# Sorting the second half of the keys' matrices ahead of the first scores, and fewer, wider warm-up matmuls

## The chip, the cores and the metric

The kernel runs on one core of one Trainium2 chip. A core has five engines with a queue of instructions each: TensorE (matmuls; the profile calls the matmuls PE and the loads of their stationary operand PEld), VectorE (DVE), ScalarE (ACT), GpSimd (POOL, which here also issues most of the loads) and SyncE (SP, which issues DMAs). They run side by side and wait for each other through semaphores. SBUF holds the working data, PSUM takes the results of matmuls. DMAs move data between HBM and SBUF; the engines' instructions too are fetched from HBM, by a DMA queue that the profile lists as "instruction".

The metric is the time of one execution in microseconds (us). Before the change it was 359.16 us, the median of 3 runs (359.14 to 359.62).

## The reference, cut to what matters

Four batches, 8 heads, 768 tokens in 8 blocks of 96, head size 64. A matrix of 8 x 8 for each batch and head is normalised five times over (Sinkhorn), then mixes the blocks of k and v; each block of queries attends to its own mixed block; the result goes through four experts of two layers whose outputs are summed with the token's weights.

```
P = sort_net
for _ in range(5):
    P = exp(P - max(P, -1)); P = P / sum(P, -1); P = P / sum(P, -2)
k_sorted = einsum('bhij,bhjcd->bhicd', P, k_b); v_sorted = the same of v_b
attn = softmax(scale * q_b @ k_sorted^T); x = attn @ v_sorted
out = sum over e of p[:, e] * (relu(x @ w1[e]) @ w2[e])
```

## The kernel before

The order of the work is written out by hand: the instructions of each engine run in the order in which the program emits them. The change lies in the first 15 us, the work on batch 0 up to the first experts.

**Warm-up.** `warm(n)` (L256) emits n matmuls of a constant tile `dummy` with itself, 128 columns each, whose result nobody reads. `warm(84)` stands first in TensorE's queue (L280). In the fifth round of the normalisation come the transposes of the first half of the queries (`h_q`, 2 x 24, L285 to 287), then `warm(30)` (L288). In the trace a matmul is a weight load and a matmul, two instructions.

**The sort matrices.** VectorE and ScalarE normalise `sn` in five rounds (L283 to 299). Then VectorE and GpSimd write a widened copy `sn16`, four of the eight block rows each (L303). `r_half(a)` (L314) turns one half by 4 matmuls against the identity into PSUM (`ps_R`, seen as `Rv`). For the first half VectorE at once builds the mixing operand `PI0[0]` from `Rv` (L354). The second half is needed as a copy in SBUF, `Rs`, from which GpSimd builds `PI0[1]` (L1375); later batches use `Rs` as well. `ps_R`, the warm-up tiles, `ps_mk` and others take turns in a pool of two PSUM buffers, so the second tile after `ps_R` (that of `mk1`) can't be written before `Rs` has been copied out.

**The first stage of batch 0.** Heads come in two quads (qd 0 and 1), output blocks in two halves (hf).

- `mix_half(nm, qd, hf)` (L485) mixes k or v by 24 matmuls; 8 keep-warm matmuls stand ahead of the first one (L481). `mixed` (L503) copies the product out, in two pieces for k of quad 0 (`mk0`: ScalarE, block rows 0-1 and 2-3) and v of quad 0 (`mv0`: VectorE).
- `h_s(qd, qq)` (L540): 8 matmuls of scores, then ScalarE's exponential into `ET` (L556).
- `h_w` (L517): transposes of mixed v, copied out by VectorE (L527).
- `h_a` (L561): 8 matmuls of attention times v; VectorE divides (L580, L581). With `later` the division is emitted afterwards.
- `h_x(qq, copy, qds)` (L590): 4 matmuls for each quad that turn the result into `xT`, and a copy out (L602).
- `group0(qq, nq, g, kcs)` (L666): the first expert's first layer, 16 matmuls of 192 columns for two kc; ScalarE's relu.

The program after the first half's `PI0` (L1365 on) is: mk0, its first copy, mv0, its first copy, `h_s(0, 0)`, `r_half(1)`, mk0's second copy on ScalarE, `Rs` on VectorE, GpSimd's loads and `PI0[1]`, `h_w(0)`, mv0's second copy, mk1 with two copies, `h_a(0, 0)`, `h_w` of the other two rows ("w01"), `h_s(0, 1)`, mv1, `h_x(0, [0])`, `h_s(1, 0)`, `h_w(1)`, `h_a(0, 1)`, `h_a(1, 0)`, the first `group0`, `h_w(1)` of the other rows ("w11"), `h_x(0, [1])`, and so on. From there to the end the experts' matmuls alternate with the attention of the later batches.

Of the kernel before, what the change touches and what calls it, by code (L numbers as in the profile page):

```python
# [17 lines left out]
def kernel(  # L18
# [11 lines left out]
    nc = tc.nc  # L30
# [8 lines left out]
    P = 128  # L39
# [27 lines left out]
    def psa(shape, dtype, name):  # L67
        state["n"] += 1
        return psA.tile(shape, dtype, tag="ps", name=name)
# [75 lines left out]
    def load_half_queries(hf):  # L145
        for qd in range(2):
            nc.gpsimd.dma_start(
                q0[ds(64 * qd, 64), hf].rearrange("p h r d -> p h (r d)"), half_queries(qd, hf)
            )

    dummy = Hflat[:, ds(2 * NFC * 2 * P, P)]
# [77 lines left out]
    def spread_weights():  # L229

        nc.vector.tensor_reduce(p_den, p_in, AX.X, ALU.add)
        yield
        nc.vector.tensor_scalar(out=p_den, in0=p_den, scalar1=1e-9, scalar2=None, op0=ALU.add)
        yield
        nc.vector.reciprocal(p_den, p_den)
        yield
        nc.vector.tensor_tensor(
            p_out.rearrange("p e t -> p t e"), p_in, p_den.broadcast_to([P, NT, E]), ALU.mult
        )
        p_rows = p_dram.rearrange("e (p t) -> p e t", t=NT)  # L240
        nc.sync.dma_start(p_rows[0:S_P], p_out[0:S_P])
        nc.sync.dma_start(p_0, p_dram[0, 0:S].rearrange("(t p) -> t p", p=P))
        pbs[(0, 0)] = load_p(0, 0)
        nc.sync.dma_start(p_rows[S_P:P], p_out[S_P:P])
        yield
# [10 lines left out]
    def warm(n):  # L256
        ps = psM.tile([P, 4, P], F32, tag="ps", name=f"ps_w_{state['n']}")
        state["n"] += 1
        for m in range(n):
            nc.tensor.matmul(ps[:, m % 4, :], dummy, dummy, start=True, stop=True)  # L260

    qT0 = [from_spare(2 * S).rearrange("p (s f r x) -> p s f r x", s=2, f=2, r=R) for _ in range(2)]

    def h_q(qd, hf, copy):

        ps = psa([P, 2, R, 64], F16, f"ps_q_{qd}_{hf}")
        rows = ds(64 * qd, 64)
        for sg in range(2):
            for r in range(R):
                for hh in range(2):  # L270
                    nc.tensor.transpose(
                        ps[ds(D * hh, D), sg, r, :], q0[rows, hf, 2 * sg + hh, r, :], ident[rows, rows]
                    )
        copy(qT0[qd][:, :, hf], ps[:])
# [2 lines left out]
    srow = const.tile([GH, NB, 1], F32, name="srow")  # L277
    scol = const.tile([GH, NB, 1], F32, name="scol")
    sn16 = const.tile([GH, NB, NB, CP], F16, name="sn16")
    warm(84)  # L280
    p_steps = spread_weights()
    nc.gpsimd.tensor_copy(ident6, ident[0:R, 0:R])
    for it in range(5):  # L283
        nc.scalar.activation(sn[:], sn[:], AF.Exp, bias=0.0, scale=1.0)
        if it == 4:  # L285
            for qd in range(2):
                h_q(qd, 0, nc.scalar.copy)
            warm(30)  # L288
        nc.vector.tensor_reduce(srow[:], sn[:], AX.X, ALU.add)
        nc.vector.reciprocal(srow[:], srow[:])  # L290
        nc.vector.tensor_tensor(sn[:], sn[:], srow[:].broadcast_to([GH, NB, NB]), ALU.mult)
        nc.vector.tensor_reduce(scol[:], sn[:].rearrange("p i j -> p j i"), AX.X, ALU.add)
        nc.vector.reciprocal(scol[:], scol[:])
        if it < 4:
            nc.vector.tensor_tensor(
                sn[:], sn[:],
                scol[:].rearrange("p j o -> p o j").broadcast_to([GH, NB, NB]),
                ALU.mult,
            )
            if it:  # L300
                next(p_steps)
# [10 lines left out]
    Rv = ps_R[:, :, 0:HB * GH].rearrange("p a (i g) -> p a i g", g=GH)  # L312

    def r_half(a):  # L314
        for i in range(HB):
            nc.tensor.matmul(
                Rv[:, a, i, :], sn16[:, a * HB + i, :, :].rearrange("g j c -> g (j c)"),
                ident[0:GH, 0:GH], start=True, stop=True,
            )
# [4 lines left out]
    Rs = const.tile([P, GH, NB], F16, name="Rs")  # L324
# [31 lines left out]
    vec, act = nc.vector.tensor_copy, nc.scalar.copy  # L356
# [128 lines left out]
    def mix_half(nm, qd, hf, pool, warm_up=0):  # L485

        ps = pool([P, 1024], F32, f"ps_m{nm}_{qd}_{hf}")
        keep_warm(ps[:, 0:P], warm_up)
        tails[(nm, qd, hf)] = ps[:, 2 * R * 64:1024].bitcast(F16).rearrange("p (n x) -> p n x", n=2)
        ps = ps[:, 0:2 * R * 64].rearrange("p (s r x) -> p s r x", s=2, r=R)  # L490
        for sg in range(2):
            for r in range(R):
                for hh in range(2):
                    h = 4 * qd + 2 * sg + hh
                    nc.tensor.matmul(  # L495
                        ps[ds(D * hh, D), sg, r, :],
                        head(0, nm, h)[:, r, :],
                        PI0[hf][:, h, :, :].rearrange("p i c -> p (i c)"),
                        start=True, stop=True,
                    )  # L500
        return ps

    def mixed(nm, qd, ps, i0, n, copy):  # L503

        dst = kTs[qd][:, 0:S] if nm == "k" else vT0[qd]
        copy(
            dst.rearrange("p (i x c) -> p x i c", i=HB, c=CP)[:, :, ds(i0, n)],
            ps.rearrange("p s r (i c) -> p (s r) i c", c=CP)[:, :, ds(i0, n)],
        )
# [30 lines left out]
    def h_s(qd, qq, ps=None):  # L540

        kT, ET = kTs[qd], ETs[2 * qd + qq % 2]
        if ps is None:
            ps = psa([P, 2, 512], F32, f"ps_s0_{qd}_{qq}")
        for n in range(4):
            for hh in range(2):
                sg, i = n // 2, 2 * (qq % 2) + n % 2

                m = BLK if 2 * i + sg == 3 else P
                nc.tensor.matmul(  # L550
                    ps[0:m, hh, ds(n * BLK, BLK)],
                    kT[ds(D * hh, D), ds((2 * i + sg) * BLK, m)],
                    qT0[qd][ds(D * hh, D), sg, qq // 2, :, ds((2 * (qq % 2) + n % 2) * CP, CP)],
                    start=True, stop=True,
                )
        nc.scalar.activation(  # L556
            ET[:, 0:S].rearrange("c (h x) -> c h x", h=2), ps[0:BLK, :, 0:HS],
            AF.Exp, bias=0.0, scale=SCALE,
        )
# [806 lines left out]
    mixed("k", 0, mk0, 0, 2, act)  # L1366
    mv0 = mix_half("v", 0, 0, psa)
    mixed("v", 0, mv0, 0, 2, vec)
    h_s(0, 0)
    r_half(1)  # L1370
    mixed("k", 0, mk0, 2, 2, act)
    vec(Rs.rearrange("p g (a i) -> p a g i", a=2), Rv.rearrange("p a i g -> p a g i"))
    load_half_queries(1)
    load_w2(0, 2)
    build_PI0(nc.gpsimd, 1, 0, H, Rs[:, 0:H, HB:NB])  # L1375
# [160 lines left out]
```

## Time and profile before

| what | before |
|---|---|
| median of 3 runs | 359.16 us (359.14 to 359.62) |
| profiled execution: from its first to its last instruction (span) | 357.8 us |
| profiled execution: its own time | not listed beside its span; the runs' median is 1.3 us above the span |
| TensorE matmuls, weight loads | 3949 and 3949 |
| TensorE busy | 351.6 us, 98% of the span |
| packets of the instruction queue q8 | 31, together 0.51 MB |
| granted TensorE clock | full from 5.99 us, not granted in full before |

A timeline line reads: start, duration, engine, line of the program, operation, output tile <- input tiles, shape, count, and in brackets how long the engine sat idle before it and what ended that. A matmul's duration includes its run through the array, so rows of matmuls overlap. "issue" as a releaser means that no semaphore and no engine shown by the profile explains the idle time.

### The profile page before, as it was taken

The page shows a single profiled execution, that of the slowest core. Times are in us where ns is not written, and L with a number is a line of the kernel's source. Part 1 is how long each engine was busy: PE and PEld are TensorE (multiplying, and loading weights), DVE is VectorE, ACT ScalarE, POOL GpSimd, SP SyncE. Part 2 cuts the span into 40 slices and gives each one's busy share as a digit, 9 for nine tenths or more (in the row PEclk, how much of TensorE's full clock was granted, in tenths as well). Part 3 has the DMA queues.
Part 4 walks back from the last instruction along what each step waited for, and adds up shares of the span by engine and source line. Part 5 has one row for each costly group of instructions (what it writes and reads, how often), then busy time and mean ns, then how long its engine had stood idle before and what let it go on. Part 6 is the DMA issues. An engine that isn't in the chain of part 4 may idle for free.

```text
span 357.8 us, 9498 instructions
## 1 busy us (share of the span) xinstructions
PE 351.6 (98%) x3949; PEld 306.3 (86%) x3949; DVE 276.2 (77%) x552; ACT 170.6 (48%) x303; POOL 133.6 (37%) x149
## 2 busy tenths in 40 slices
PE   8899999999999999999999999999999999999996
PEld 8686867888888888888899988888888888888886
DVE  5754797869889587868978988896678886588963
ACT  2554240442434535367947258830288611688201
POOL 8864010375122222000535318840058800188400
PEclk9999999999999999999999999999999999999999
DMA  8999999999999999935996420005200015100011
GB/s 114 207 205 228 216 210 198 209 163 165 201 154 160 188 152 170 194 74 73 168 201 90 102 78 0 2 2 108 102 29 2 3 39 138 61 0 2 2 73 46
DMA packets 72022, 40.51 MB, mean 113 GB/s; under 512 B 40614, under 2 KB 66732, under 8 KB 71980
## 3 DMA queue, kind: packets, MB, share of 16 engines
q0 software_dynamic: 36576, 19.93, 41.9%
q1 hardware_dynamic: 35260, 19.92, 28.5%
q8 instruction: 31, 0.51, 0.6%
q14 instruction: 11, 0.09, 0.1%
q10 hardware_dynamic: 144, 0.07, 0.1%
HBM read 42.13 MB, written 6.34 MB: 135 GB/s over the span
## 4 chain that ended last, share of the span: by engine, by line
PE 95%; DVE 2%; ACT 1%; DMA 0%; issue 0%; DVEq 0%
PE ps_h L790 18%; PE ps_Q L1264 18%; PE ps_p L774 12%; PE ps_X L1121 10%; PE ps_Z L1121 7%; PE ps_Q L1121 7%; PE ps_Z L1264 6%; PE ps_h L679 3%; PE ps_o L714 3%; PE ps_p L830 3%; PE ps_a L453 2%; PE ps_s L418 2%; PE ps_k L399 1%; PE ps_v L365 1%; PE ps_a L567 1%; PE ps_mk L495 1%
## 5 line engine op out<-in xcount | busy, mean ns | idle before, releaser
L790 PE MATMUL ps_h<-xT,w 128*128 128x256 f16 x576 | 67.5, 273 | 0.0
L790 PEld LDWEIGHTS <-w 128*128 128x128 f16 x576 | 55.2, 98 | 7.2
L796 DVE SCALAR_TENSOR_TENSOR Hb<-ps_h,pb 128x1024 f16<-128x1024 f32 x34 | 41.5, 1223 | 17.2 <-PE ps_h L790 15.8
L1121 PEld LDWEIGHTS <-w 128*128 128x128 f16 x480 | 43.6, 98 | 4.8
L1134 POOL TENSOR_TENSOR arena<-tmp,pb 128x512 f16<-128x512 f32 x12 | 15.2, 1275 | 65.7 <-PE ps_Z L1121 49.8
L1264 PEld LDWEIGHTS <-Hb 128*128 128x128 f16 x320 | 31.1, 98 | 3.5
L1133 ACT ACTIVATE tmp<-tmp 128x512 f32<-128x512 f32 x46 | 29.0, 632 | 3.9 <-DVE tmp L1171 3.9
L1264 PEld LDWEIGHTS <-Sb 128*128 128x128 f16 x304 | 28.3, 98 | 3.0
L1121 PEld LDWEIGHTS <-arena 128*128 128x128 f16 x312 | 27.7, 98 | 2.9
L425 ACT ACTIVATE ET<-ps_s 96x768 f16<-96x768 f32 x24 | 18.0, 802 | 25.1 <-PE ps_s L418 24.8
L121 POOL DMA_DIRECT2D arena<-in_q_dram x24 | 19.9, 838 | 25.5 <-DMA q_ring<-arena 25.2
L408 ACT CAST kT<-ps_k 64x384 f16<-64x384 f32 x48 | 22.7, 473 | 13.3 <-PE ps_k L399 12.3
L1121 PE MATMUL ps_X<-ET,arena 128*128 128x256 f16 x168 | 25.2, 272 | 0.0
L1264 PE MATMUL ps_Q<-w,Hb 128*128 128x256 f16 x192 | 24.6, 273 | 0.0
L774 PEld LDWEIGHTS <-Hb 128*128 128x128 f16 x232 | 21.8, 98 | 3.0
L1127 DVE SCALAR_TENSOR_TENSOR Hb<-ps_X,pb 128x512 f16<-128x512 f32 x27 | 18.7, 691 | 7.0 <-PE ps_X L1121 7.0
L1141 ACT COPY ps_X<-ps_Z 128x512 f32<-128x512 f32 x27 | 15.4, 571 | 17.8 <-PE ps_Z L1121 17.8
L1121 PE MATMUL ps_Z<-xT,w 128*128 128x256 f16 (+1 forms) x176 | 22.5, 258 | 0.0
L760 DVE TENSOR_TENSOR Sb<-Hb 128x512 f16<-128x512 f16 x33 | 20.6, 647 | 0.0
L1148 ACT COPY tmp<-ps_X 128x512 f32<-128x512 f32 x26 | 15.2, 585 | 9.2 <-PE ps_X L1121 6.6
L1127 DVE SCALAR_TENSOR_TENSOR Hb<-ps_Z,pb 128x512 f16<-128x512 f32 x27 | 18.4, 682 | 1.3 <-PE ps_Z L1121 1.3
L1171 DVE TENSOR_TENSOR tmp<-ps_Q,tmp 128x512 f32<-128x512 f32 x26 | 17.8, 683 | 0.8 <-PE ps_Q L1121 0.8
(266 smaller groups left out, 741.6 us busy)
## 6 DMA issues: line engine op xcount, KB each, us to landing
w<-in_moe_w_dram POOLq DMA_DIRECT2D x6, 1024.0 KB, 27.9
pb<-p_dram SPq DMA_DIRECT2D x9, 512.0 KB, 7.0
arena<-in_k_dram POOLq DMA_DIRECT2D x8, 384.0 KB, 9.3
arena<-in_v_dram POOLq DMA_DIRECT2D x8, 384.0 KB, 7.5
vs<-arena SPq DMA_DIRECT2D x36, 66.0 KB, 4.9
arena<-in_q_dram POOLq DMA_DIRECT2D x24, 96.0 KB, 7.5
out_dram<-ob SPq DMA_DIRECT2D x9, 256.0 KB, 2.0
w<-in_moe_w_dram POOLq DMA_DIRECT2D x4, 512.0 KB, 12.5
```

The lines of the kernel that those rows point to most:

```text
L121: nc.gpsimd.dma_start(t[:, h // 2, :, h % 2, :], q[b, h].rearrange("(t p) d -> p t d", p=P))
L408: nc.scalar.copy(kT[ds(D * hh, D), r], pk[ds(D * r, D), hh].rearrange("p a (i c) -> p a i c", c=CP),)
L425: nc.scalar.activation(ETs[2 * (pr % 2) + hh][:, 0:S].rearrange("c (a x) -> c a x", a=2), pss[hh][0:BLK, :, 0:HS], AF.Exp, bias=0.0, scale ...
L760: tt(sm[0], blk(0, 1), blk(1, 1), ALU.add)
L774: nc.tensor.matmul(ps, lhs(e, f), Ts[e][rhs][:, f, :], start=(first and e == es[0] and f == 0), stop=(done and e == es[-1] and f == KH - 1 ...
L790: nc.tensor.matmul(ps[:, f, :], w1sb[e][:, kc, ds((4 * g + f) * P, P)], xT[:, kc, ds(2 * c * P, 2 * P)], start=(kc == 0), stop=(kc == NKC ...
L796: nc.vector.scalar_tensor_tensor(out=Hb[:, homes.get(e, e), ds(4 * g, 4), :], in0=ps[:], scalar=0.0, op0=ALU.max, in1=weights(e).broadcast ...
L1121: nc.tensor.matmul(dst[:, ds(f * cols, cols)], a[lhs][:, k, ds((f0 + f) * P, P)], t[rhs][:, k, :], start=(first and f == 0 and k == 0), st ...
L1127: nc.vector.scalar_tensor_tensor(out=home(i, j), in0=src.rearrange("p (f x) -> p f x", f=m), scalar=0.0, op0=ALU.max, in1=weight(j).broadc ...
L1133: nc.scalar.activation(src, src, AF.Relu, bias=0.0, scale=1.0)
L1171: tt(t12, Q, u2, ALU.add)
L1264: nc.tensor.matmul(ps, lhs(e, f), Ts[e][rhs][:, f, part], start=(first and e == 0 and f == 0), stop=(e == E - 1 and f == KH - 1), skip_gro ...
```

## The change

`warm` emits matmuls of 512 columns: the moving operand is the same tile of 128 columns, read four times over, and the output is the whole buffer of 4 x 128. It is called with 21 and 8 instead of 84 and 30. `r_half(1)` moves ahead of `h_s(0, 0)` in TensorE's queue. The copy `Rs` moves from VectorE, where it stood behind mv0's first copy, to ScalarE, where it stands between mk0's first copy and the exponential of `h_s(0, 0)`. GpSimd's queue and SyncE's are as before.

```
         for m in range(n):
-            nc.tensor.matmul(ps[:, m % 4, :], dummy, dummy, start=True, stop=True)
+            nc.tensor.matmul(
+                ps[:], dummy, dummy.rearrange("p (o x) -> p o x", o=1).broadcast_to([P, 4, P]), start=True, stop=True
+            )
...
-    warm(84)
+    warm(21)
...
-            warm(30)
+            warm(8)
...
     mixed("v", 0, mv0, 0, 2, vec)
+    r_half(1)
+    act(Rs.rearrange("p g (a i) -> p a g i", a=2), Rv.rearrange("p a i g -> p a g i"))
     h_s(0, 0)
-    r_half(1)
     mixed("k", 0, mk0, 2, 2, act)
-    vec(Rs.rearrange("p g (a i) -> p a g i", a=2), Rv.rearrange("p a i g -> p a g i"))
     load_half_queries(1)
```

## The prediction

> **What bounds the kernel now.** First the page: busy shares and the chain.
>
> ```profile
> PE 351.6 (98%) x3949; PEld 306.3 (86%) x3949; DVE 276.2 (77%) x552; ACT 170.6 (48%) x303; POOL 133.6 (37%) x149
> ...
> q8 instruction: 31, 0.51, 0.6%
> ...
> PE 95%; DVE 2%; ACT 1%; DMA 0%; issue 0%; DVEq 0%
> ```
>
> TensorE bounds. The waits of TensorE from 20.3 us to the end hold one row, the stall that ends at 20.27:
>
> ```profile
> PE ps_s L522 <- issue: 0.2, 1, 0.2
> ```
>
> So after 20.3 TensorE runs without a gap, and what its queue is late or early there, the end is. The change can only count ahead of that. TensorE's timeline there:
>
> ```profile
> 8.97 1.85 PE L260 MATMUL ps_w<-Hb 128*128 128x128 f16 x30
> 11.79 0.26 PE L316 MATMUL ps_R<-ident,sn 32*128 32x32 f16 x4 [0.98 <-DVE sn L304]
> ...
> 13.78 0.21 PE L550 MATMUL ps_s<-Sb,kT 64*128 64x96 f16 x1 [0.19 <-ACT kT L506]
> 14.17 0.33 PE L550 MATMUL ps_s<-Sb,kT 64*128 64x96 f16 x7 [0.18 <-issue]
> ...
> 17.23 0.34 PE L598 MATMUL ps_a<-perm,xsl 96*128 96x96 f16 x4
> ...
> 19.85 0.22 PE L522 MATMUL ps_s<-ident,Sb 128*96 128x128 f16 x1
> 20.27 0.37 PE L522 MATMUL ps_s<-ident,Sb 128*96 128x128 f16 x3 [0.20 <-issue]
> 20.47 0.34 PE L598 MATMUL ps_a<-perm,xsl 96*128 96x96 f16 x4
> ```
>
> The warm-up ends in an idle second: r_half(0) waits for VectorE. Two stalls of 0.39 and 0.41 us (13.78 to 14.17, 19.85 to 20.27) stand within groups whose data are there: "issue". Numbering TensorE's records in order of time, they fall behind the 449th and the 705th, 256 apart. The 31 packets of q8 hold 16.4 KB each, and 31 x 256 is nearly all of TensorE's 7,945 records. So I read: instructions come in blocks of 256, the first boundary is behind record 193 (in the query transposes, at 8.37 us), and the stalls are blocks that come late. The DMA packets confirm it: q8's start at 11.786, 17.861 and 23.894 us and take 0.95, 0.94 and 0.97. The stalls end 1.44 and 1.47 us after the first two have ended, and the second and third start 3.69 and 3.63 us after the stalls have ended. So: on entering a block TensorE asks for the one after it, no earlier, and that can be used 3.66 + 0.95 + 1.45 = 6.06 us later. Thirty-one crossings and 31 packets fit two blocks being there at the start.
>
> The Trainium skill (Runtime: NRT & Kernel Launch, Instruction fetch mechanics) states blocks of 256 instructions too, fetched while the one before runs, and crossing "mostly hidden". The two stalls here were not hidden. By that rule alone the sum below would be that of the first rival, 358.7 us.
>
> **The change part by part.**
>
> *Warm-up.* 114 pairs of weight load and matmul become 29: 85 pairs, 170 instructions, go. Columns stay: 84 x 128 = 21 x 512, and 30 x 128 = 3,840 against 4,096. The trace starts these matmuls every 0.107 us until the clock is granted at 5.99 us, then every 0.056; a 512-column one of the second layer starts every 0.216 when warm, and cold it should take 4 x 0.107 = 0.43. From 1.06: 11.6 cold, 9.4 warm, end at 8.03 instead of 8.09. The eight take 1.73 instead of 1.68. The idle second until 11.79 takes both: 0. Bounds: no gain, since VectorE ends that wait; no loss until the clock comes some 2 us later (each us of half speed costs half a us), which nothing in the trace suggests at equal columns.
>
> *The boundaries.* Everything behind the warm-up stands 170 records earlier in its blocks. The first boundary falls behind old record 363, mk0's seventh load. mk0's first matmul waits for VectorE's PI0 (released at 12.60), so TensorE crosses at about 12.68, not during the warm-up as before (11.79 less 3.66 is 8.1). That it cannot run ahead through a wait: twice in the trace a sequencer record eight instructions behind a waiting one (17.150 and 67.002 us) came 0.05 us after that one's release (17.102, 66.955), though its own semaphore had long come. The next block is then usable at 12.68 + 6.06 = 18.74. It is needed behind old record 619, inside h_x(0, [0]): in program order its third load is the last of the old block, and its third matmul (17.32 us in the trace) starts at 18.74: **+1.42**.
>
> The Trainium skill (Perfetto Trace Analysis, Tensor Engine Instruction) has matmuls wait in a hardware queue while the sequencer goes on. If that queue were deep, the crossing would come about 11.8 at r_half(0) or before; that is the second rival or the first.
>
> *What is queued behind.* h_x's copy on ScalarE (17.61, 0.48), then exp of h_s(1, 0) (starts 0.375 behind the copy's start, released 0.82 later), h_a(1, 0), VectorE's division (0.96 from h_a's release), h_x(0, [1]). These are the rows of ScalarE's and VectorE's timelines:
>
> ```profile
> 17.61 0.48 ACT L602 CAST xT<-ps_a 128x384 f16<-128x384 f32 x1
> 17.98 0.81 ACT L556 ACTIVATE ET<-ps_s 96x768 f16<-96x768 f32 x1
> ...
> 18.48 0.42 DVE L527 COPY Sb<-ps_mv 96x512 f16<-96x512 f16 x1 [0.26 <-PE ps_mv L522]
> 19.39 0.20 DVE L580 RECIPROCAL rz<-ps_a 96x8 f32<-96x8 f32 x1 [0.49 <-PE ps_a L567]
> 19.63 0.69 DVE L581 TENSOR_TENSOR xsl<-ps_a,rz 96x512 f16<-96x512 f32 x1
> ```
>
> The fourth matmul, at 17.365 before, comes at 18.78 and is released at 19.00; copy 19.03; exp 19.40, released 20.22; h_a(1, 0) 20.27 instead of 18.95: +1.31 (0.1 less, since VectorE's evacuation, 18.91 before, no longer comes last). The division ends 1.31 later; h_x(0, [1]) then follows it directly, where it stood 0.05 behind: +1.26 at old 20.47. The old stall at 19.85 goes, but the division (old 20.33) lay over it: 0.07 of the 0.41, counted here. First weights' second half lands at 21.18, needed at 21.68 and now later: 0.
>
> *Next boundaries.* Third: entered 18.74, usable 24.80; needed behind old record 875, in h_x(1, [1]) at old 24.68, now 25.94: hidden. The next is asked for there: usable 25.94 + 6.06 = 32.00, needed behind old record 1131, a 512-column matmul of the second layer whose successor, at old 30.44, is due at 31.70: **+0.30**. Then: asked for at 32.0, usable at 38.1, needed at old 39.9: hidden. From 45 us on the packets are 7 to 17 us apart, more than 6.06: 0 (0 to 0.2).
>
> *The reorder.* r_half(1) needs GpSimd's sn16, released at 12.66; it can run behind mv0 (13.6) where TensorE idles 0.19: 0. Rs on ScalarE: nearest rows 0.48 (128x384 from PSUM there) and VectorE's own 0.42 for the same copy; by size 0.39, bounds 0.26 (a 32x64 activation) and 0.48. It delays exp(0, 0) by up to that against a first score without its stall: exp would start 14.33 instead of 14.54. mk1 no longer waits 0.23 for VectorE's Rs. Without late blocks h_x(0, [0]) would be reached 0.42 us sooner: mv0's first copy ends at 14.19, so h_w(0) could start at 14.25 instead of 14.62 and VectorE's evacuation of it at 14.73 instead of 15.15; mv0's second copy, w01, h_s(0, 1), mv1 and h_x follow each other from there (17.23 to 16.8). With the block usable at 18.74 all this ends in the same wait: 0. GpSimd's PI0[1] needs Rs by 15.39, when its loads are issued, and Rs is there by 14.5: 0. No DMA is moved.
>
> Sum: 1.26 + 0.30 = 1.56 us. The profiled execution's span goes from 357.8 to 359.4; the median of the runs stands 1.3 above that span: 359.16 + 1.56 = **360.7**.
>
> **The rivals.**
>
> 1. *Blocks are in time* (other side). If TensorE crosses by 10.7 us, during the warm-up, the block is usable at 16.8, when h_x(0, [0]) is reached. Then the 0.39 at 13.78 goes, the reorder brings h_x 0.42 forward, and from 20.3 it stays: 358.7 (358.4 to 359.1). For it: records run up to 34 ahead in steady stretches. Against: the two records held behind a wait. It decides up to 10.7 (16.8 less 6.06); from 11.2 the wait has eaten the 0.42.
> 2. *Crossing at r_half(0)*: 34 ahead of execution, record 159 is reached at 11.8. Usable 17.9, +0.6 in h_x, 0.42 at 20.47, 0.3 at the later boundary: 359.9 (359.6 to 360.1).
> 3. *A crossing costs a fixed 0.4, whenever.* Then one in mk0 replaces that of h_s(0, 0); one in h_x is mostly seen (0.1 to 0.3), one at old 24.7 (0.35), and 0.07 is won: 359.6 (359.2 to 359.9). Against: at 19.85 the load's data had come at 19.42, and a fixed 0.4 would have been over by 19.87.
> 4. *The clock falls* in the longer wait of 1.5 us: half speed for some us, +1 to 3. Against: after the idle 0.98 at 10.8 the keep-warm matmuls of 11.99 still start 0.056 apart.
>
> **How the numbers follow.** Chances: late blocks as worked out 0.62, rival 1 0.16, 2 0.12, 3 0.06, 4 0.04. The likeliest one's own range: the asking lag was 3.63 and 3.69, and 4.05 if the first crossing ran 34 ahead; 3.43 and 3.78 for the next two: +1.0 to +1.65 for the first, 0.05 to 0.55 for the second wait: 360.2 to 361.4. The range reaches down over rivals 2 and 3 to the middle of rival 1: 358.7 to 361.4. A measurement of this kernel tells about 0.2%, 0.72 us, from no change: slower is above 359.88 (0.62 less a little, a third of rival 2, rival 4: 0.68), faster below 358.44 (rival 1's edge: 0.05), same 0.27.
>
> **What would show it.** Warm-up rows x21 and x8, ending near 8.2 and 10.9. q8's first packet near 16.3 us instead of 11.8, the second near 22.4, the third near 29.7. No issue stall at h_s(0, 0); one of some 1.5 us inside h_x(0, [0]) ending near 18.7; none at the w11 transposes; a short one near 32 in the second layer; no gap behind. h_x(0, [1]) near 21.8. First packet at 12 to 14 us and no stall: rival 1. Wrong also, if the compiler gave TensorE a few more or fewer instructions, which moves the boundary out of h_x (by up to five either way it stays).

## The result, and the profile after

The changed kernel takes 360.86 us (median of 22 runs, 360.34 to 362.48); the kernel before, beside it on the same chip, takes 359.62 (22 runs, 359.14 to 361.97). The ratio is 1.0035, with a 95% interval of 1.0023 to 1.0046: slower by about 1.24 us. The fastest executions differ as much: 360.34 against 359.14. The forecast was 360.7. Of all executions named below, one, with 58 pairs, took 518 us at a granted clock of 0.66 and is left out.

The profiled execution of the changed kernel took 361.94 us, 1.78 above its span of 360.16. The later profiles have 1.77 to 1.86 between span and time too. So the profiled execution of before, with its span of 357.84, took about 359.62, and the prediction's base of 359.16 belonged to faster executions than the one it had read.

First the page of the changed kernel: busy shares, the instruction queue, the chain.

```profile
PE 352.0 (98%) x3864; PEld 301.6 (84%) x3864; DVE 276.1 (77%) x551; ACT 171.0 (47%) x304; POOL 133.7 (37%) x149
...
q8 instruction: 30, 0.49, 0.6%
...
PE 92%; DVE 3%; DMA 2%; SPq 1%; issue 1%; ACT 1%; DVEq 0%
```

85 matmuls and 85 loads are gone, and one code packet with them. TensorE is still 98% busy, but the chain now holds 2% of DMA and 1% of SPq, where before it had neither to speak of. What DMA that is comes below. TensorE's timeline, up to the second transposes (start, duration, line, operation, tiles, count, idle before):

```profile
1.06 6.35 PE L260 MATMUL ps_w<-Hb 128*128 128x512 f16 x21 [1.06 <-DVE Hb L152]
...
8.12 1.90 PE L260 MATMUL ps_w<-Hb 128*128 128x512 f16 x8
11.73 0.26 PE L318 MATMUL ps_R<-ident,sn 32*128 32x32 f16 x4 [1.71 <-DVE sn L306]
...
16.77 0.26 PE L600 MATMUL ps_a<-perm,xsl 96*128 96x96 f16 x2
18.26 0.32 PE L600 MATMUL ps_a<-perm,xsl 96*128 96x96 f16 x2 [1.23 <-issue]
...
21.97 0.34 PE L600 MATMUL ps_a<-perm,xsl 96*128 96x96 f16 x4
```

The stall is where the prediction put it: h_x(0, [0]) starts its first two matmuls at 16.77, and the third waits for nothing but its own instruction until 18.26. q8's first three packets start at 15.77, 22.06 and 29.00 us. The two stalls of before are gone. h_x(0, [1]) runs at 21.97, 1.50 us later than at 20.47 before.

Part of those 1.50 us is the clock. The same execution by stretches (start:end, length, busy time and count of each engine, granted clock, DMA share, GB/s):

```profile
core 0: us, PE busy (x) PEld busy (x) DVE busy (x) ACT busy (x) POOL busy (x), PEclk, DMA share, GB/s
...
18.00:21.50 3.50, 3.24 (x39) 2.97 (x39) 0.93 (x3) 1.72 (x3) 1.48 (x4) 0.51 1.20 204
21.50:24.00 2.50, 2.50 (x41) 2.26 (x39) 1.83 (x5) 1.19 (x2) 2.23 (x4) 1.00 1.25 207
```

The granted clock is half from 18.07 us, 0.19 ahead of the end of the stall, to 21.49, then full again. At the third matmul the lag is 0.94 (17.32 before, 18.26); with the slower clock it is 1.54 when the old transposes of 20.27 run. And there is a wait that before does not have anywhere behind 20.3 us; the waits of TensorE from 20.3 us to the end:

```profile
PE ps_a L455 <- DMA vs<-arena: 0.4, 1, 0.4
```

It ends at 181.18 us and takes the lag to 2.05. `vs` is a tile of mixed v for a later batch. ScalarE copies the product out into a part of `arena` (L371 before, L373 after), SyncE (SP) moves it into `vs` by six DMAs (L379, now L381), and TensorE multiplies with it (L453, now L455). The span is longer by 2.32 us, 0.30 more than the lag of TensorE's last matmul; where that comes from, the run with the new order alone shows.

### The profile page after: what moved, and what is told of

Same layout as the page of the kernel before. It is cut to its first block, busy times and chain, and to the rows that moved or that the text cites. A ratio compares the mean times of both kernels' runs of the same rounds, so it can differ in the third digit from the quotient of the medians.

```text
span 360.2 us, 9329 instructions
## 1 busy us (share of the span) xinstructions
PE 352.0 (98%) x3864; PEld 301.6 (84%) x3864; DVE 276.1 (77%) x551; ACT 171.0 (47%) x304; POOL 133.7 (37%) x149
## 4 chain that ended last, share of the span: by engine, by line
PE 92%; DVE 3%; DMA 2%; SPq 1%; issue 1%; ACT 1%; DVEq 0%
PE ps_h L792 18%; PE ps_Q L1266 17%; PE ps_X L1123 10%; PE ps_p L776 10%; PE ps_Z L1123 7%; PE ps_Q L1123 7%; PE ps_Z L1266 6%; PE ps_h L681 3%; PE ps_o L716 3%; PE ps_p L832 3%; DMA vs<-arena 2%; PE ps_a L455 1%; PE ps_s L420 1%; PE ps_k L401 1%; SPq L381 1%; PE ps_v L367 1%
## 5 line engine op out<-in xcount | busy, mean ns | idle before, releaser
L1266 PE MATMUL ps_Q<-w,Hb 128*128 128x256 f16 x192 | 24.6, 273 | 0.0
L1173 DVE TENSOR_TENSOR tmp<-ps_Q,tmp 128x512 f32<-128x512 f32 x26 | 17.8, 683 | 0.8 <-PE ps_Q L1123 0.8
```

The lines of the kernel that those rows point to most:

```text
L1173: tt(t12, Q, u2, ALU.add)
L1266: nc.tensor.matmul(ps, lhs(e, f), Ts[e][rhs][:, f, part], start=(first and e == 0 and f == 0), stop=(e == E - 1 and f == KH - 1), skip_gro ...
```

## The experiments

All twelve runs compute the whole reference; the warm-up matmuls that some of them add give results that nobody reads. Shifts below are starts of the same TensorE instruction in the new profile less its start in the first profile of before. "h_x(0,[1])" is at 20.47 there. Batches of runs had their own runs of the kernel before beside them; its median was 359.5 to 359.6 each time.

### One half of the change at a time

Only the warm-up, in the old order:

```
-                nc.tensor.matmul(ps[:, m % 4, :], dummy, dummy, ...)
+                nc.tensor.matmul(ps[:], dummy, <dummy read four times over>, ...)
...
-    warm(84)
+    warm(21)
...
-            warm(30)
+            warm(8)
```

> Only the warm-up of the change (21 and 8 matmuls of 512 columns), the order of the sort matrices as before. Theory 'late block': the whole loss is here. TensorE enters its second block of instructions only in the first mix at about 12.66 us, the next block can be used 5.6 to 6.1 us later, and a stall without a data reason ends between 18.2 and 18.8 us inside h_x(0, [0]); before + 0.9 to 1.4 us, no issue stall at the first scores. Rival 'order': the loss comes from Rs standing on ScalarE ahead of the first exponential, then this kernel is as before (within 0.2 us). Rival 'clock': the loss is a fall of the granted clock in the wait; then the loss goes with the record of the clock (0.6 us where it falls for 3.4 us, else nothing beyond the stall).

Measured: 360.97 us, ratio 1.0034 (1.0016 to 1.0052). TensorE's timeline in h_x, then its waits from 20.3 us on:

```profile
16.85 0.26 PE L600 MATMUL ps_a<-perm,xsl 96*128 96x96 f16 x2
17.72 0.24 PE L600 MATMUL ps_a<-perm,xsl 96*128 96x96 f16 x2 [0.61 <-issue]
...
20.68 0.34 PE L600 MATMUL ps_a<-perm,xsl 96*128 96x96 f16 x4
```

```profile
PE ps_a L455 <- DMA vs<-arena: 1.1, 1, 1.1
PE ps_s L420 <- ACT arena L373: 0.3, 1, 0.3
```

The warm-up alone carries the whole loss. But the stall is only 0.61 us here and leaves 0.21 at h_x(0,[1]); the clock stays full. Most of this execution's lag comes later: it goes to 0.70 at 162.15 us, where ScalarE's copy into `arena` is late, and to 1.92 at 181.05, where `vs` is late.

Only the new order, with the 114 matmuls of 128 columns as before:

```
     mixed("v", 0, mv0, 0, 2, vec)
+    r_half(1)
+    act(Rs...)
     h_s(0, 0)
-    r_half(1)
     mixed("k", 0, mk0, 2, 2, act)
-    vec(Rs...)
```

> Only the order of the change, with the 114 warm-up matmuls of 128 columns of before. Theory 'late block': the boundary behind record 449 now lies in r_half(1), its stall ends at about 14.2 us as before, the next one again at the w11 transposes at about 20.2 us, where TensorE waited before too; so before + 0.0 (-0.1 to +0.2 us). Rival 'order': before + 0.9 to 1.4 us.

Measured: 359.74 us, ratio 1.0006 (0.9992 to 1.0021). Neither of the two stalls on issue that were expected is there; h_x(0,[0]) starts at 16.85, and h_x(0,[1]) at 20.00:

```profile
20.00 0.34 PE L598 MATMUL ps_a<-perm,xsl 96*128 96x96 f16 x4
```

h_x(0,[1]) is 0.47 early, and TensorE's last matmul is still 0.45 early; yet the span is 357.94, not shorter. In this execution the time from VectorE's last addition to the end, with the last write of the output, was 0.55 longer than in the first profile of before. The second queue of code, q14, has one packet more within the span, and the last write took longer from its issue to its landing (lines of the page and of the view of that write, in us); first before, then the new order:

```profile
q14 instruction: 11, 0.09, 0.1%
...
DMA to landing us min/median/max: 1.6/1.6/1.6
```

```profile
q14 instruction: 12, 0.10, 0.1%
...
DMA to landing us min/median/max: 2.2/2.2/2.2
```

This is no chance of one execution. In all eight profiles with the new order a packet of q14 starts 1.26 to 1.41 us after the start of TensorE's last matmul, while that write is under way, the write takes 1.9 to 2.2 us, and the end comes 3.65 to 3.99 us after that start. In all six with the old order that packet starts only after the end of the span, the write takes 1.6, and the end comes after 3.38 to 3.42. ScalarE has one instruction more in the new order (304 against 303, `Rs`), which would move a boundary of its code; that this is what brings the packet forward, and the packet what delays the write, is argued and not shown. So the order gains 0.45 us in front and loses 0.55 at the end, and in the sum nothing can be measured.

### How many instructions: 89, 58 and 42 pairs

In these the warm-up keeps about its time, but some matmuls stay at 128 columns, so that fewer instructions go. Sketch for 89 pairs in the new order (`warm(n, wide)` emits n of 128 columns and then `wide` of 512):

```
-    warm(84)
+    warm(59)
...
-            warm(30)
+            warm(22, 8)
```

> The order of the change, with 89 warm-up matmuls instead of 29 or 114: 59 of 128 columns first, then 22 of 128 and 8 of 512, so about the same columns and the same time. Theory 'late block': the first boundary is crossed at about 7 us, the next block can be used at about 13, and is needed inside mk1 at about 14.6: no issue stall there; the one after is asked for at about 14.7, can be used at 20.3 to 20.8 and is needed at about 21: none or under 0.1 us. No issue stall at all ahead of 25 us, TensorE reaches h_x(0, [1]) at about 20.0 us instead of 20.47, before - 0.45 us (-0.6 to -0.2). Rival 'order': slower than before by 0.9 to 1.4 us, since the order is that of the change. Rival 'width': between before and the change.

> The order of before with the 89 warm-up matmuls of the run with the new order. Theory 'late block': no issue stall either, before - 0.4 us (-0.55 to -0.15); the new order by itself is worth 0.05 us (mk1 no longer waits for Rs, but the chain over VectorE's copies of mixed v is hardly shorter). If the order were worth more, this kernel would be 0.2 us or more behind the one with the new order.

89 pairs in the new order: 360.01 us, 1.0012 (1.0000 to 1.0024). In the old order: 359.53, 0.9997 (0.9981 to 1.0012). A gain of 0.4 us and more was expected of both, and neither shows it. Neither has a stall on issue up to 24 us. The profile of the first has other waits instead: 0.39 us for the v load before 13.61, 0.31 for the first weights before 22.26. That v load is issued at 4.04 to 4.13 us in every kernel, and landed between 10.8 and 13.6 us over the profiles.

Then the two that should find the edge:

```
-    warm(21)
+    warm(30, 14)      # 58 pairs       warm(16, 17)   # 42 pairs
...
-            warm(8)
+            warm(9, 5)                 warm(2, 7)
```

> The changed kernel with 58 warm-up pairs in place of 29: 30 of 128 columns and 14 of 512 in the first group, 9 and 5 in the second, about the same time in all. 112 TensorE instructions fewer than in the kernel before, so the first boundary lies at the third pair of the second group, crossed at about 8.5 us. Late block: with the lags seen so far (2.6 to 3.9 us until the block's first packet, 0.95 for it, up to 1.6 until it can be used) the next block can be used by 13.7 to 15.0 us and is needed at about 16.1; the one behind it is needed at about 23.1 and there by 22.5. No wait on issue between 12 and 24 us, time 359.6 to 360.1 beside 359.5 for the kernel before. If it is the wide matmuls themselves (the clock, or what 512 columns do to it) that cost, 19 of the 29 are still there and it takes 360.3 to 360.9. If the loss grows evenly with the number of instructions taken away, 112 of 170 give 0.7 to 0.9 us: 360.2 to 360.4.

> The changed kernel with 42 warm-up pairs in place of 29: 16 of 128 columns and 17 of 512 in the first group, 2 and 7 in the second. 144 TensorE instructions fewer than in the kernel before: the first boundary lies two pairs behind the last of the four transposes of r_half(0), crossed at 11.9 to 12.1 us, since that one waits for VectorE's sn until 11.73. Late block: usable at 17.2 to 18.5 us, needed at about 16.5 in the mix of mv1: a wait on issue of 0.7 to 1.5 us there, in another tile than in the changed kernel, and 360.2 to 361.0 us. If TensorE's sequencer reads past the waiting transpose by tens of instructions, the boundary is crossed at about 10.7, the block is there by 16.9 and the wait is under 0.4 us, 359.6 to 360.0. If the loss grows evenly with the number of instructions taken away: 144 of 170 give 1.0 to 1.2 us with no wait on issue in one place.

58 pairs: 360.87 us (11 runs), ratio 1.0044 (1.0025 to 1.0063). 42 pairs: 360.50, 1.0023 (1.0014 to 1.0032). Neither matches the theory of the late block. The times alone speak for its rivals: by the intervals 58 pairs lose 0.9 to 2.3 us, where the wide matmuls were given 0.7 to 1.3 and a loss that grows with the instructions taken away 0.7 to 0.9, and 42 pairs lose 0.5 to 1.15, where the latter was given 1.0 to 1.2. With 58 pairs the front is as good as it gets (h_x(0,[1]) at 19.99, 0.48 early, no stall on issue), and the kernel is as slow as the changed one. TensorE's waits from 20.3 us on, with 58 pairs:

```profile
PE ps_h L794 <- DVE Hb L800: 0.5, 1, 0.5
PE ps_s L422 <- ACT arena L375: 0.2, 1, 0.2
```

The lag goes from -0.48 to +0.24 at 98.06 us and to +0.68 at 162.12, and the end with the last write is 0.56 longer than before. At 98 us VectorE had waited for a 512 KB load (pb) of SP's queue, which landed at 96.69 (96.29 before). So there is a loss that needs no stall in front. With 42 pairs there is no stall on issue at all; q8's first packet starts at 11.62 us, 0.18 before r_half(0) runs. The new block begins 11 instructions behind r_half(0)'s waiting first load, and in the other 13 profiles the first packet started 2.5 to 3.9 us after the instruction at the boundary ran; here 0.44 before. So TensorE had asked for it before the wait was over: it does read at least 11 instructions past a waiting one. What this execution waits for is loads:

```profile
16.68 0.57 PE L499 MATMUL ps_mv<-Sb,arena 128*64 128x64 f16 x24 [0.26 <-DMA arena<-in_v_dram]
...
21.91 0.83 PE L683 MATMUL ps_h<-xT,w 128*128 128x192 f16 x8 [0.30 <-DMA w<-in_moe_w_dram]
```

### The two kernels once more

No edit; second profiles.

> The changed kernel once more, for a second profile of it. Late block: a wait on issue of 0.8 to 1.4 us ahead of the third matmul of h_x(0,[0]), at about 17.3 of the kernel before, with the granted clock full throughout, and h_x(0,[1]) 0.6 to 1.0 us later than in the kernel before; 360.3 to 360.7 us where vs<-arena is in time at 181 us and 1.1 us more where it is not. If the fall of the clock is part of the change, it is there again from about 18 us and adds 0.5 us at h_x(0,[1]).

> The kernel before once more, for a second profile of it, to see what of a shift between two profiles is in neither's edit. Waits on issue at the same two records, 13.8 to 14.2 and 19.9 to 20.3 us, h_x(0,[1]) within 0.2 us of the first profile, no wait for vs<-arena at 179 us or one of up to 1.1 us, since some runs of this kernel take 1.1 to 1.7 us more than its median.

The changed kernel: 361.39 us (5 runs, 360.85 to 361.81; ratio 1.0043, 1.0028 to 1.0058). Its timeline and its waits from 20.3 us on:

```profile
17.70 0.24 PE L600 MATMUL ps_a<-perm,xsl 96*128 96x96 f16 x2 [0.60 <-issue]
...
20.66 0.34 PE L600 MATMUL ps_a<-perm,xsl 96*128 96x96 f16 x4
```

```profile
PE ps_s L420 <- ACT arena L373: 0.7, 1, 0.7
PE ps_a L455 <- DMA vs<-arena: 0.3, 1, 0.3
```

The same stall in the same place, but of 0.60 us where the first profile had 1.23. It leaves +0.19 at h_x(0,[1]); the clock does not fall. The lag then goes to 1.10 at 162.55 and 1.60 at 180.73. The fall of the clock is no fixed part of the change: of the 22 runs only the profiled one has a mean clock below 0.998, and two of the 35 runs of the kernel before that stood beside the first four experiments have 0.994 and 0.995.

The kernel before: one run, 359.50. It has neither of the two stalls on issue from which the prediction read the blocks; q8's first packet starts at 11.42 instead of 11.79, and that is enough. It waits 0.34 us for the first weights instead, and ends within 0.11 us of its first profile's span. Its chain holds 4% of DMA, so that share, too, moves with nothing changed.

### What makes vs late

SP needs about 0.6 us to issue one of the six DMAs, and in the changed kernel some issues take longer. The issues of `vs` around 155 us, first before, then the changed kernel's second profile, then 58 pairs (minimum/median/maximum of six in ns, start of the first and last):

```profile
L379 SPq DMA_DIRECT2D vs<-arena x6: 577/594/600, 154.2 to 157.4; - x6
```

```profile
L381 SPq DMA_DIRECT2D vs<-arena x6: 577/596/1875, 154.4 to 157.6; - x6
```

```profile
L383 SPq DMA_DIRECT2D vs<-arena x6: 577/598/1397, 154.5 to 158.5; - x6
```

One issue took 1.88 us, one 1.40. Laid beside q8's packets, the fifth of the six runs of issues (154 to 161 us) gives a clean picture over all 14 profiles, 84 issues: in four of them a code packet starts between 0.37 us ahead of the issue's start and 0.11 behind it, and these four take 1.88, 1.46, 1.40 and 0.94 us. The other 80 take at most 0.61; among them are five in which a packet starts 0.27 to 0.41 us into the issue. In before the packets next to this run start at 151.8 and 162.1, clear of it; taking 170 instructions out moves them to 157.6 to 159.3, and 112 to 155.5. In the sixth run (169 to 177 us) some issue of 0.96 to 1.42 us stands in every profile, in before too, mostly with no packet near; in the two profiles of the changed kernel and in that of the warm-up alone a packet at about 172 us falls there, and two issues in a row are long (with before and 43 cut, below, the packet falls there too and one is long). Over all six runs of issues in the 14 profiles, 504 issues, 18 have a packet in that window of 0.37 ahead to 0.11 behind: 16 of them take 0.94 to 1.88 us, two 0.57 and 0.59. In the first, second, third and sixth run issues of over 0.7 us occur without such a packet too.

To take the place of the late packets apart from the front, matmuls of the second layer (512 columns) were cut into narrower ones with the same columns: more instructions behind 28 us, none ahead. The core of it:

```
-                nc.tensor.matmul(ps, h0(fc)[...], w2sb[0][:, fc, :], ...)
+                for s in range(k):   # k = 2: 512 columns as two of 256
+                    nc.tensor.matmul(ps[:, ds(s * w, w)], h0(fc)[...], w2sb[0][:, fc, ds(s * w, w)], ...)
```

> The kernel before with 43 of the 48 matmuls of the second layer (second_layer0, 28.5 to 57 us, 512 columns each) cut into two of 256 columns: the same columns, 86 TensorE instructions more, and every boundary behind 57 us at the same instruction as in the changed kernel, since 86 and 170 add up to 256. Nothing ahead of 28 us is touched. Theory of the late fetches: the code block that TensorE fetches at about 157.6 us and the one at about 172 us fall into SP's runs of six vs<-arena issues, as in the changed kernel; one issue takes 0.9 to 1.9 us in place of 0.60, ScalarE or TensorE waits at about 162 us (0.2 to 0.7) and TensorE for vs<-arena at about 181 us (0.3 to 1.1): 360.2 to 361.3 us beside 359.5. Theory of the late block: what the change costs is lost inside h_x, which is untouched here: 359.3 to 359.8 us, with no wait at 162 us.

> The changed kernel with all 48 matmuls of the second layer cut into two of 256 columns, and the 32 of 384 columns in the first layer (40 to 51 us) into two of 192: 160 TensorE instructions more, 10 fewer than in the kernel before, so that behind 57 us every boundary is within 10 instructions of where it is there. The front is that of the changed kernel. Theory of the late fetches: the wait on issue ahead of the third matmul of h_x(0,[0]) is there again with 0.6 to 1.2 us and leaves 0.2 to 0.9 at h_x(0,[1]), but no vs<-arena issue at 154 to 158 us takes over 0.7 us, nothing waits at 162 us, and vs is in time at 179 us: 359.5 to 360.3 us. Theory of the late block: all of the loss is in front: 360.6 to 361.4 us, as the changed kernel.

> The control for the two others: the kernel before with 24 of the 48 matmuls cut into four of 128 columns, the other 24 into two, and the 32 of the first layer into two: 256 instructions more, one whole block, so that behind 57 us every boundary is at the instruction where it was. Theory of the late fetches: no wait at 162 us and none over 0.2 us at 179 us, and 359.3 to 359.9 us if the cut matmuls cost nothing; what they do cost shows as a shift between 28 and 57 us that stays to the end. If more instructions alone cost time, twice to three times the loss of the kernel with 43 cut ones.

Before with 43 cut: 359.96 us, ratio 1.0013 (1.0002 to 1.0025). Its control with a whole block more: 360.10, 1.0022 (1.0009 to 1.0035), so more than was expected of either; in its profile the cut matmuls and a wait on issue of 0.06 use up the 0.4 us by which it was early at 24 us. So the late boundaries of the changed kernel, put into the kernel before, cost nothing measurable beyond the cutting. But in the profile they did not make the coincidence that they were to make. The packet came, at 157.62 us, but 0.32 us into the sixth issue, and no issue there was long:

```profile
L379 SPq DMA_DIRECT2D vs<-arena x6: 577/594/605, 154.1 to 157.3; - x6
```

A quarter of a us decides. The changed kernel with the late boundaries of before: 361.65, 1.0055 (1.0035 to 1.0076), no better than the changed kernel. No `vs` issue around 155 us was long and nothing waited at 162 or 181; the front was late, though not by the code:

```profile
17.68 0.57 PE L497 MATMUL ps_mv<-Sb,arena 128*64 128x64 f16 x24 [1.26 <-DMA arena<-in_v_dram]
...
22.09 0.34 PE L600 MATMUL ps_a<-perm,xsl 96*128 96x96 f16 x4
```

In this execution the second v load landed at 17.64 us (15.1 to 17.0 in the others), and the clock fell behind that wait too. The third matmul of h_x(0,[0]) followed at 18.29 without a stall of its own; with q8's packet at 15.33 and the lags above, its block was there by about 17.8, so that stall is hidden here. At 100.7 us came 0.87 us for VectorE, which waited for a 512 KB load (pb) of SP's queue. These two speak against the late packets as the main cause for itself: with the front of before they cost nothing here, and with the late front the loss stays when the packets are moved away. They don't settle it, since the first did not hit an issue in its profile and the second was late through a load.

### The same boundaries with more instructions

Last, the place of the boundary against everything else that the warm-up's change does. 86 instructions more put the boundaries where 170 fewer put them:

```
-    warm(84)
+    warm(41, 86)     # 41 of 128 columns, then 86 of 64 by 64
```

> The new order with more warm-up pairs than the kernel before, not fewer: 157, of 128 columns except for 86 of 64 by 64 in the first group (41 of 128 and 86 of 64, then 30 of 128), the same number of columns as before's 114. 86 instructions more put every boundary at the instruction where the changed kernel, with 170 fewer, has it (86 and 170 add up to a block of 256): one at mk0's seventh load, crossed at about 12.7 us, the next at the third matmul of h_x(0,[0]). Late block: a wait on issue of 0.6 to 1.3 us there, h_x(0,[1]) 0.2 to 0.9 us later than in the kernel before, the wait for vs<-arena at 181 us again, and the time of the changed kernel, 360.3 to 361.4 us beside 359.5. If the loss comes of the 512-column matmuls, or of the smaller number of instructions, this kernel has neither: no wait on issue and 359.4 to 360.0 us, as the new order with 114 pairs (359.74). If the warm-up ends later than at 11.7 us because pairs of 64 columns take more than 27 ns, r_half(0) starts late by that much, which would show ahead of 11.8 us.

Measured: 363.61 us (362.14 to 364.29), ratio 1.0104 (1.0081 to 1.0127). The timeline, with the two boundaries, and the clock:

```profile
12.65 0.28 PE L497 MATMUL ps_mk<-Sb,arena 128*64 128x64 f16 x6
13.38 0.47 PE L497 MATMUL ps_mk<-Sb,arena 128*64 128x64 f16 x18 [0.44 <-issue]
...
17.48 0.26 PE L600 MATMUL ps_a<-perm,xsl 96*128 96x96 f16 x2
19.30 0.24 PE L600 MATMUL ps_a<-perm,xsl 96*128 96x96 f16 x2 [1.56 <-issue]
...
22.99 0.53 PE L600 MATMUL ps_a<-perm,xsl 96*128 96x96 f16 x4
```

```profile
20.20:23.60 3.40, 3.40 (x38) 3.33 (x38) 1.87 (x6) 1.06 (x3) 1.75 (x3) 0.50 1.27 207
```

More matmuls than before, all narrow, and the stall is at the very instruction: ahead of the third matmul of h_x(0,[0]). A second one stands at mk0's seventh load, after six matmuls, where the boundary one block earlier lies. r_half(0) runs at 11.80, so the warm-up did not end too late. The loss is three times that of the changed kernel and 2.2 us above the range expected. Most of it, 2.5 of the 3.6 us by which this span is longer, is there at h_x(0,[1]), because the block behind mk0's seventh load is itself late here, and the next is asked for only then: 13.38 to the packet at 16.92 (3.54), 0.94 for it, 1.44 until it is used, 5.92 together. Then the clock halves from 20.23 to 23.65, and h_x(0,[1]) is 2.52 late; five of the six runs have a mean clock of 0.994 or 0.995. So neither the 512 columns nor a smaller number of instructions is needed for the stall or for a loss: the place of the boundary is enough. Whether they cost something besides, as the times with 58 pairs would allow, this run doesn't say.

## Why the prediction was right, and where not

**The forecast.** Slower by 1.56 us was forecast, and 1.24 measured. The time itself, 360.7 against 360.86, is nearer than the step deserved, since the base was 0.46 below the median of 22 runs. That it came out is in part luck: of the two terms of the sum 0.30 did not occur, and 1.26 was 0.19 in the profile in which the clock stayed full, while 162 to 181 us and the last write, both put at nothing, brought 1.4 and 0.6 there.

**Warm-up at nothing: right.** It ends at 10.0 us (10.9 forecast; the full clock came at 4.42 here) and VectorE ends the wait at 11.73, as before (11.79). The start of the full clock moves on its own, between 3.7 and 6.7 us over the profiles, and r_half(0) runs at 11.73 to 11.81 in all of them.

**A late block inside h_x(0, [0]): right in place.** Three profiles with that boundary and 29 pairs, and one with 157, stall ahead of the third matmul (in a fifth the load's wait covers it); those with 42, 58, 89 or 114 pairs don't. The step on when TensorE crosses was wrong: "it cannot run ahead through a wait". With 42 pairs it read 11 instructions past one. In the changed kernel the new block begins 37 behind r_half(0)'s wait and 12 behind mk0's, so it was likely crossed when r_half(0) was released, at 11.73, not at 12.68. That was the premise of rival 2, which put the block at 17.9; the stall ended at 18.26, 17.70 and 17.72. The crossing itself no profile shows. The Trainium skill (Perfetto Trace Analysis, Tensor Engine Instruction) has the sequencer go on while matmuls wait in a queue; these 11 instructions agree with it, and the prediction set it aside on two records.

The Trainium skill (Runtime: NRT & Kernel Launch, Instruction fetch mechanics) calls a crossing mostly hidden. That agrees with 42, 58, 89 and 114 pairs in the new order, where no wait on issue stands ahead of 24 us, and not with 29 and 157, where 0.60 to 1.56 us were seen.

**The size: +1.42 at the third matmul was 0.94 and 0.38.** The term that was mis-sized is the sum of 6.06 us from 12.68: 5.58 and 5.02 were measured from there. Its parts behind the packet's start held: 0.89 to 0.95 for the packet, 1.38 to 1.60 until it was used. What follows from h_x to h_x, +1.26 forecast, was +1.50 with the clock's fall and +0.19 without it. When the stall is 0.6, the old stall of before at 20.27 that is gone pays for half of the lag of 0.38 at the third matmul.

**The second wait, +0.30 near 32 us: wrong.** No profile has it. q8's second packet (asked for at 18.26, started at 22.06) was usable at about 24.6 and the third, started at 29.00, at about 31.5, just ahead of its use at about 31.7.

**"What its queue is late there, the end is": wrong.** This is the step that failed most. It held in the other direction, of before, in which nothing waits behind 20.3 us. In the changed kernel's two profiles 0.5 and 1.4 us of the lag at the end come at 162 and 181 us (1.7 with the warm-up alone), from `vs<-arena`, and 0.3 and 0.6 us more lie in the last write, behind TensorE's last matmul. No rival had a DMA that was comfortable before and late after: what a moved code fetch delays elsewhere was never asked.

**The reorder at nothing: right in the sum, as a balance that was not seen.** h_x(0, [0]) is reached at 16.77 (16.8 forecast), Rs takes 0.37 on ScalarE (0.39), and the order alone is not measurably slower or faster. But without a late block it gains 0.45 us at TensorE's last matmul and gives 0.55 back in the last write; "No DMA is moved" left out the code packet of q14.

**The rivals.** 1, blocks in time, did not happen at this boundary; where it did (114 pairs in the new order, 89 in the old) the 0.46 to 0.47 won at 20 us did not reach the median, so 358.7 would have been too low. 4, the clock falls, happened in the first profile, for 0.6 us and not 1 to 3, and by the mean clocks in none of the other 21 runs; "against" was argued from an idle second that ended without it. 3, a fixed 0.4, falls with stalls of 0.44 to 1.56.

**What stays open.** The profiled executions of the changed kernel took 361.94 and 361.77 us, above its median of 360.86. How the loss divides between the front, 162 to 181 us and the last write in an execution of 360.5 is not shown, and so the late block is shown as the cause of the stall, not of the whole 1.24 us. The two experiments that separate front and late packets say that the late packets alone cost nothing, and that the front alone is enough, but in the profile of the first no issue was hit, and that of the second was late through a v load. Why 58 pairs lose 1.3 us with a good front is shown only in one profile, by waits at 98 and 162 us and by the last write; that wide matmuls or a smaller number of instructions cost something there is not excluded.

## What to carry to other kernels

Removing instructions that run for free can cost time, since it moves every later boundary of code blocks: number the engine's instructions, see which ones the boundaries fall on before and after, and look for one that is crossed shortly behind a wait with less than some 6 us (5.0 to 6.1 here) of work in the next 256 instructions. For a change of a third of a per cent one profile is not enough: the two stalls that carried this reading were absent from the second profile of the same kernel, and the changed kernel's stall was 1.23 us in one and 0.60 in the other. Other engines' code moves as well: one instruction more on ScalarE went with a later end in all eight profiles. And when a queue has no idle time, look for the transfers that were only just in time: a lag in front does not simply pass through to the end.

## What the runs showed of the hardware

- A code packet of TensorE (16.4 KB) that starts within 0.37 us ahead of an SP DMA issue or 0.11 behind its start goes with an issue of 0.94 to 1.88 us instead of 0.6: four of four in the fifth run, 16 of 18 over all `vs` issues. A packet 0.27 to 0.41 us into an issue goes with none in that run. This is a coincidence in time; nothing shows the mechanism.
- The granted clock went to half for 3.41 us in the three profiles with a wait of TensorE of 1.23, 1.26 (for a load) and 1.56 us that ended between 17.7 and 19.3 us, and not with 0.60 and 0.61 there. It fell between 0.19 us ahead of the end of the wait and 0.93 behind it, each time 13.65 us, four times 3.41, after the full clock had begun (4.42, 4.60 and 6.58 us). In front, 1.7 to 2.1 us of idle just ahead of 11.8 us left it full.
- TensorE reads ahead past a waiting instruction by at least 11 instructions, with 42 pairs; the prediction's two records, eight behind a wait, were no limit.
- A packet of the code queue q14 that starts 0.7 to 0.8 us after the issue of the last write goes with 1.9 to 2.2 us from that issue to its landing (eight profiles), none there with 1.6 (six).
- The same load, issued at the same time (5.5 us), landed between 15.1 and 17.6 us over 14 profiles.
